# Attention and two expert layers on one core: pairs in column quarters, strays by register addresses, all work by a fixed list

## The chip, the cores and the metric

The kernel runs on 1 core of one Trainium2 chip. The metric is the device time of one execution in microseconds (us). The kernel before takes 580.2 us, the median of 3 runs (579.23 to 580.48).

In this text PE is TensorE, DVE is VectorE, ACT is ScalarE, POOL is GpSimd, SP is SyncE (here it issues nearly all DMAs).

## What is computed

Random-feature attention over 4 batches of 8 heads with 576 tokens, 64 wide, and then two layers of 8 experts, each token to the expert with the largest gate:

```python
def _attn_ref(q, k, v, omega):
    m, D = omega.shape                       # 128 features, 64
    scale = 1.0 / np.sqrt(np.sqrt(D))
    q_s, k_s = (q * scale, k * scale)
    def phi(x):
        proj = np.einsum('bhsd,md->bhsm', x, omega)
        sq = np.sum(x * x, axis=-1, keepdims=True) / 2.0
        h = proj - sq
        h = h - np.max(h, axis=-1, keepdims=True)
        return np.exp(h) / np.sqrt(m)
    q_p, k_p = (phi(q_s), phi(k_s))
    kv = np.einsum('bhsm,bhsd->bhmd', k_p, v)
    z = np.sum(k_p, axis=2)
    num = np.einsum('bhsm,bhmd->bhsd', q_p, kv)
    den = np.einsum('bhsm,bhm->bhs', q_p, z)[..., None] + 1e-06
    return (num / den).astype(np.float32)

def _moe_ref(x, w_gate, w_output_gate, w1, w2):      # x: 2304 x 512, F = 1024, 8 experts
    logits = x @ w_gate
    e_idx = np.argmax(logits, axis=1)
    ...                                              # gate_w: softmax value of the chosen one
    eom = 1.0 / (1.0 + np.exp(-(x @ w_output_gate)))
    for e in range(E):
        mask = e_idx == e
        h = np.maximum(x[mask] @ w1[e], 0.0)
        out[mask] = gate_w[mask, None] * eom[mask, e, None] * (h @ w2[e])
    return out
```

The second layer is the same without the output gate `eom`. The output is the second layer's, kept transposed on the chip as `outT` (512 x 2304).

## The kernel before

**Attention.** A *pair* is two heads of a batch; there are 16, and each has a form (`FORMS`, line 54). All forms project k on 64-row tiles (`k_proj`, line 487): 10 fp32 matmuls, 20 records in the trace, into `ph`; then a maximum (`nm`), and an exponential for each 128 columns (`kp`). q is projected too, its maximum over features is taken by POOL (`partition_all_reduce` into `qhl`), DVE subtracts, ACT takes the exponential. The forms differ in three steps:

- F (5 pairs): `kv` (line 493) as ten fp32 matmuls 128x128, `num` (line 530) as four fp32 matmuls 128x288 into `pa`, features by tokens.
- R (3 pairs): `kv` in four 32-column quarters of the array, 40 matmuls 32x65 into `pkv`; `num` with token rows, again 40 matmuls 32x65 into `pn` (`rows`, line 548), a division by the sum's column, and five transposes `pf` back to features by tokens.
- S (8 pairs): like F, but q and `kv` are cut in a high and a low part in fp32r, and `num` has three terms per half (`qh`·`kvh`, `ql`·`kvh`, `qh`·`kvl`); q's projection takes two terms (`qs` with `omsth` and `omstl`).

In F and S the denominator is a row of `num`; it goes out by DMA to `rdd`, comes back as `rb` on 64 rows, and `norm` multiplies (`xraw<-ev,rb`).

**Expert layers.** Nearly all tokens of a batch choose one expert in each layer. A *unit* is one layer of one batch with its majority expert. `Unit.up` (line 936) has 8 chunks, each 24 fp32r matmuls `pm` (128x288, three terms `xh`·`wh`, `xl`·`wh`, `xh`·`wl`) into one tile of two banks, 576 columns; ACT makes `hh` by relu from all 576 columns, DVE makes the rest `hl`. `Unit.down` (line 963) has 4 chunks of 48 matmuls, whose result DVE multiplies by the tokens' weights `cb` into `y`. 8 units of 384 make 3072 `pm`. The weights come raw as `wr`, ACT casts them to `wh`, DVE makes `wl`, 1024 columns at a time.

**Gates and strays.** Per unit `gate` (line 769) computes logits (`pg`, `pt`), counts (`pc`) and the weights' table (`ptc`, to DRAM as `cohd`). Tokens of another expert than the unit's, the *strays*, are taken by `Block` (line 1035), `JB` = 32 at a time: selection by `sel`, transposes of all tokens (`pst`, `pxt`), a gather by matmul (`pxg`, `pxf`), up (`pu`, `phf`), down (`pyc`), and a scatter by matmul with the table `put` (`pby`). The result `by` is merged into the last unit's `y`, or added to another batch's output (`old`) that is read back. The first block always runs; further ones run in a loop behind the main program, only if the counts ask for it.

**Order.** A planner (`Estimate`, line 102) models each engine's time as the program is written; between the chunks of a unit a `slot` (in `run_unit`, line 1389) lets in the next attention step, gate step or store, by weights, paces and tweaks (lines 58 to 70). Where nothing is ready before the first unit, `fill` issues matmuls `idle` on zeros.

**PSUM.** 8 banks: 7 for attention and 1 for `idle` before the first unit; then two `pm` tiles of two banks and 4 for the rest.

Of the kernel before, what the change touches and what calls it, by code (L numbers as in the profile page):

```python
# [2 lines left out]

# [10 lines left out]
I32 = mybir.dt.int32  # L14
AF = mybir.ActivationFunctionType
# [10 lines left out]
NCH = 5  # L26
# [7 lines left out]
BW = 96  # L34
BN = S // BW
JB = 32
# [13 lines left out]
)  # L50
ORDER = 3


FORMS = "FRRRFFFSFSFSSSSS"
CW = 132
XW = 4

WEIGHTS = (-99.0, -99.0, 465.22, -215.23, 475.57, 303.97, 62.0, -391.59, -72.09, 241.12, -272.33, 415.93, -220.17, 177.53)
RAW_WEIGHTS = (-99.0, -99.0, -320.83, -643.41, 757.51, 23.54, 902.27, -181.77, -108.58, 760.71, -209.95, -1003.88, -544.16, -272.35)
# [40 lines left out]


class Estimate:

    def __init__(self):
        self.now = dict.fromkeys(("tensor", "vector", "scalar", "gpsimd", "sync", "dma"), 0.7)
        self.written, self.used, self.slots, self.before = {}, {}, {}, {}
        self.sums = set()

        self.banks, self.seen, self.uses = {}, {}, 0

        self.window, self.work, self.slow = 0, 0.0, True

        self.holds = []

        self.rows = 128

    def ready(self, tiles):
        return max((self.written.get(t.tensor.name, 0.0) for t in tiles), default=0.0)  # L120

    def tile(self, ring, bufs, t):


        names = self.slots.setdefault(ring, [])
        if len(names) >= bufs:
            old = names[0]
            if self.banks.get(ring):
                read = [n for n in names if n in self.seen and not self.seen[n][1]]
                old = min(read, key=lambda n: self.seen[n][0], default=old)  # L130
            names.remove(old)
            self.before[t.tensor.name] = old
        names.append(t.tensor.name)

    def spare(self, pool, tag):

        ring = id(pool), tag
        return pool.bufs - sum(n not in self.seen or self.seen[n][1] for n in self.slots.get(ring, ()))

    def clock(self, begin):  # L140
        while begin >= (self.window + 1) * 3.413:
            if self.slow:
                self.slow = self.work < 0.77 * 3.413
            else:
                self.slow = self.work < 0.4 * 3.413
            self.window += 1
            self.work = 0.0
        return 2 if self.slow else 1

    def run(self, engine, op, out, ins):  # L150
        n = math.prod((ins[0] if "reduce" in op and ins else out).shape[1:])
        free = self.used.get(self.before.get(out.tensor.name), 0.0)
        begin = max(self.now[engine], self.ready(ins), free)
        psum = any(t.tensor.name in self.sums for t in (out, *ins))
        if op == "dma_start":
            self.now[engine] = begin + (0.42 if out.shape[0] % 128 == 0 else 0.55)
            row = out.shape[-1] * 4
            cost = math.prod(out.shape[:-1]) / 16e3 * (2 + row / 25 if row >= 512 else 40 if row > 256 else 10)
            if len(out.shape) > 2 and row >= 512 or out.shape[0] == 64:
                cost *= 1.5  # L160
            end = self.now["dma"] = max(begin + 1.1, self.now["dma"]) + max(0.17, cost)
            end += 1.0
        elif engine == "tensor":
            if op == "transpose":
                cost, tail = max(n, 128) / 1185, 0.17
            elif ins[-1].dtype == F32:

                cost, tail = 2 * max(2 * n / 2400 + 0.002, 0.111), 0.1
                cost *= 0.5 if ins[-1].shape[0] == 64 else 0.25 if out.shape[0] == 32 else 1
            elif ins[-1].dtype == F32R:  # L170
                cost, tail = n / 2400 + 0.0112, 0.165
            else:
                cost, tail = n / 2400 + 0.0025, 0.165
            rows = 64 if ins[-1].shape[0] == 64 else 32 if out.shape[0] == 32 else 128
            if rows != self.rows:
                begin += 0.1
                cost += 0.107
                self.rows = rows
            cost *= self.clock(begin)
            self.work += cost  # L180
            end = self.now[engine] = begin + cost
            end += tail + 0.045
        else:
            if engine == "gpsimd":
# [4 lines left out]
            elif engine == "vector":  # L189
# [8 lines left out]
                for h in self.holds:  # L198
                    if h < begin < h + 1.2 and not psum:
                        begin = h + 1.2  # L200
# [70 lines left out]

# [1254 lines left out]
```

## Time and profile before

| | |
|---|---|
| median of 3 runs | 580.2 us (579.23 to 580.48) |
| the profiled execution | 578.27 us, its span 576.4 us |
| mean granted PE clock | 0.994 |
| first `pm` starts | 69.03 us |
| last `pm` starts | 569.73 us |
| last store issued | 571.10 us |

The rows come from the one profiled execution; times in them are from the span's start. PE is busy nearly all the time, so its rows are read as a sum of durations by kind of work. A PE row's x counts records: an fp32 matmul leaves two. Records overlap, so the time that a visit costs is taken from one start to the next start.

### The profile page before, as it was taken

Reading aid. Unit: us, or ns where it says so; the run is one execution under the profiler, and the core shown is the slowest. Engines: PE = TensorE matmul, PEld = TensorE weight load, DVE = VectorE, ACT = ScalarE, POOL = GpSimd, SP = SyncE. Lnnn points to the kernel's source line nnn. Section 1 sums busy time; section 2 is a strip of 40 time slices with the busy share of each in tenths; the row PEclk is TensorE's granted clock in tenths of the full one; section 3 lists DMA queues with packets and bytes.
Section 4 is the critical chain, followed back from the end, with each engine's and each line's share of the span. In section 5 each row is a group of like instructions: output and inputs, shape, how many; then the busy total and the mean of one; then the engine's idle time right before and its main releaser. Section 6 shows DMA issues by size and latency. Waiting matters only on the chain.

```text
span 576.4 us, 12103 instructions
## 1 busy us (share of the span) xinstructions
PE 561.6 (97%) x4859; PEld 532.5 (92%) x4859; DVE 365.1 (63%) x685; ACT 222.5 (39%) x503; POOL 68.6 (12%) x48
## 2 busy tenths in 40 slices
PE   8989999999999999999999999999999999999995
PEld 7768789999899999999999999999999999879994
DVE  3696678976976887697686865445544575314522
ACT  5967556332445433522445313312421332224300
POOL 3743400121111111020131000000000000000000
PEclk9989999999999999999999999999999999999998
DMA  8323476636546263373545363533333337964411
GB/s 309 119 85 129 107 233 167 197 98 179 162 116 188 80 200 113 100 241 111 156 118 142 123 196 94 131 135 115 95 115 116 94 96 226 314 204 133 120 42 45
DMA packets 96958, 82.81 MB, mean 144 GB/s; under 512 B 24576, under 2 KB 78464, under 8 KB 96896
## 3 DMA queue, kind: packets, MB, share of 16 engines
q1 hardware_dynamic: 95776, 81.78, 46.6%
q8 instruction: 40, 0.66, 0.5%
q10 hardware_dynamic: 1120, 0.19, 0.2%
q14 instruction: 22, 0.18, 0.1%
HBM read 66.36 MB, written 15.54 MB: 142 GB/s over the span
## 4 chain that ended last, share of the span: by engine, by line
PE 75%; DVE 5%; ACT 1%; issue 1%; ACTq 0%
PE pm L229 62%; PE pa L229 4%; PE pkv L229 3%; PE ph L229 2%; PE pg L229 1%; DVE hl L229 1%; DVE qhh L229 1%; DVE wl L229 1%; PE pby L229 1%; DVE y L229 1%; ACT wh L229 0%; PE pxt L229 0%; ACT hh L229 0%; ACT qhh L229 0%; PE pu L229 0%
## 5 line engine op out<-in xcount | busy, mean ns | idle before, releaser
L229 PE MATMUL pm<-xh,wh 128*128 128x288 f32 x512 | 114.2, 304 | 3.2 <-DVE hl L229 2.0
L229 PE MATMUL pm<-hh,wh 128*128 128x288 f32 x512 | 113.9, 301 | 0.6 <-DVE y L229 0.6
L229 PE MATMUL pm<-hh,wl 128*128 128x288 f32 x512 | 110.8, 295 | 0.0
L229 PE MATMUL pm<-hl,wh 128*128 128x288 f32 x512 | 110.8, 295 | 0.0
L229 PE MATMUL pm<-xh,wl 128*128 128x288 f32 x512 | 109.6, 296 | 0.3 <-DVE wl L229 0.3
L229 PE MATMUL pm<-xl,wh 128*128 128x288 f32 x512 | 109.4, 295 | 0.0
L229 POOL PARTITION_ALL_REDUCE qhl<-qhh x32 | 67.4, 2134 | 242.0 <-DVE qhh L229 167.2
L229 ACT CAST wh<-wr 128x1024 fp32r<-128x1024 f32 (+1 forms) x72 | 68.0, 957 | 69.4 <-PE pm L229 48.7
L229 DVE TENSOR_TENSOR wl<-wr,wh 128x1024 fp32r<-128x1024 f32 (+1 forms) x72 | 78.8, 1104 | 17.2 <-ACT wh L229 16.2
L229 PEld LDWEIGHTS pm<-xh,wh 128*128 128x128 f32 x512 | 81.9, 189 | 7.8 <-DVE hl L229 3.4
L229 PEld LDWEIGHTS pm<-hh,wh 128*128 128x128 f32 x512 | 82.5, 189 | 4.3 <-issue 2.7
L229 DVE SCALAR_TENSOR_TENSOR hl<-pm,hh 128x576 fp32r<-128x576 f32 x64 | 48.3, 754 | 59.6 <-ACT hh L229 58.9
L229 PEld LDWEIGHTS pm<-hh,wl 128*128 128x128 f32 x512 | 82.8, 188 | 0.0
L229 PEld LDWEIGHTS pm<-xh,wl 128*128 128x128 f32 x512 | 82.2, 188 | 0.6 <-DVE wl L229 0.6
L229 PEld LDWEIGHTS pm<-hl,wh 128*128 128x128 f32 x512 | 82.8, 188 | 0.0
L229 PEld LDWEIGHTS pm<-xl,wh 128*128 128x128 f32 x512 | 82.3, 188 | 0.0
L229 ACT ACTIVATE hh<-pm 128x576 fp32r<-128x576 f32 x64 | 41.9, 655 | 73.1 <-PE pm L229 73.0
L229 DVE TENSOR_TENSOR y<-pm,cb 128x576 f32<-128x576 f32 (+1 forms) x33 | 24.2, 732 | 65.7 <-PE pm L229 65.6
L229 ACT ACTIVATE kp<-ph,nm 128x128 f32<-128x128 f32 x140 | 37.7, 392 | 20.2 <-DVE nm L229 20.2
L229 ACT ACTIVATE qhh<-qhh 128x576 f32<-128x576 f32 x32 | 22.5, 719 | 34.7 <-DVE qhh L229 29.6
L229 DVE TENSOR_REDUCE nm<-ph 128x3 f32<-128x384 f32 (+1 forms) x64 | 27.0, 484 | 11.6 <-PE ph L229 9.1
L229 PE MATMUL pkv<-vt,kp 128*128 128x128 f32 (+1 forms) x400 | 32.3, 254 | 0.6 <-issue 0.3
(146 smaller groups left out, 559.0 us busy)
## 6 DMA issues: line engine op xcount, KB each, us to landing
wr<-w2a SPq DMA_DIRECT2D x16, 512.0 KB, 3.8
wr<-w2b SPq DMA_DIRECT2D x16, 512.0 KB, 4.1
qr<-qT SPq DMA_DIRECT2D x24, 288.0 KB, 4.0
wr<-w1a SPq DMA_DIRECT2D x12, 512.0 KB, 4.1
wr<-w1b SPq DMA_DIRECT2D x12, 512.0 KB, 3.8
vt<-vp SPq DMA_DIRECT2D x16, 325.0 KB, 4.6
kr<-kT SPq DMA_DIRECT2D x16, 288.0 KB, 4.0
xd<-xraw SPq DMA_DIRECT2D x16, 288.0 KB, 3.8
```

Source lines behind the costliest of these rows:

```text
L229: return f(*args, **kw)
```

## The change

All 16 pairs take form R, with q projected on 64 rows in fp32, k projected and exponentiated in two parts, and the two-part q, `kv`, and the road over `rdd` gone. A `pm` tile is one bank with 288 columns: each half of the tokens is its own group (`group`, 12 matmuls in up, 24 in down) with its own relu, `hl` or `y`. `psm` keeps two banks, `psa` has six, for the whole program. Some casts of `wh` stand on DVE (names with + in the list): 24 of 1024 columns and 8 of 512. Counts go through a bf16 matmul. `JB` is 8: DVE's maximum of eight finds the stray positions, POOL loads them into registers and copies the eight columns of x; `pu` is 16 matmuls 32x256, `phf` two transposes, `pyc` 32 matmuls 32x128, `pby` one transpose, and POOL copies the eight result columns into a cleared `by`. The planner is gone: `PLAN` is a list of steps, where a number is that many half-groups of the units' matmuls, and a name one step of a pair (its letter, the pair, the half), a gate (`G`), a weight piece (`F` load, `H` cast, `L` rest), or the block (`A`, `B`). There are 25 `idle` matmuls where there were 42.

```diff
-JB = 32
+JB = 8
-FORMS = "FRRRFFFSFSFSSSSS"
+BANKS = 2
...
+def group(nc, out, terms, ws, xs, first, last):
+    for t in terms:
+        nc.tensor.matmul(out, ws(*t), xs(*t), start=first and t == terms[0], stop=last and t == terms[-1])
...
-        def up(self, x, need, slot):
+        def run(self):
...
-                pm = pl.psm.tile([128, 2, 512], F32, tag="pm", name="pm")
...
+                for s in range(2):
+                    pm = pl.psm.tile([128, 512], F32, tag="pm", name="pm")[:, :HS]
+                    for c in (0, 2):
+                        w = self.w[fc // 2]
+                        group(
+                            nc, pm, [(d, *t) for d in (c, c + 1) for t in TERMS],
...
+                    nc.scalar.activation(hh[:, s], pm, AF.Relu)
+                    nc.vector.scalar_tensor_tensor(
+                        out=hl[:, s], in0=pm, scalar=0.0, in1=hh[:, s].bitcast(F32), op0=ALU.max, op1=ALU.subtract
+                    )
+                    yield
...
+            nc.vector.max(out=top, in_=sel)
...
+                t = nc.gpsimd.value_load(at[0:1, j : j + 1], min_val=0, max_val=S)
+                nc.gpsimd.tensor_copy(out=xg[:, :, j : j + 1], in_=x[:, :, bass.ds(t, 1)])
...
+                nc.gpsimd.tensor_copy(out=by[:, :, bass.ds(t, 1)], in_=yw[:, :, j : j + 1])
...
-    psums = ExitStack()
-    pl.psa = pool(psums, "psa", 7, space=PSUM)
-    pl.psi = pool(psums, "psi", 1, space=PSUM)
+    pl.psm = pool(ctx, "psm", BANKS, space=PSUM)
+    pl.psa = pool(ctx, "psa", 8 - BANKS, space=PSUM)
...
+        for name in PLAN.split():
+            if name.isdigit():
+                for _ in range(int(name)):
+                    next(experts)
+            elif name[0] == "z":
+                spin(int(name[1:]))
+            elif name in flows:
+                next(flows[name], None)
```

Of the list, the end:

```
H75 2 L75 3 F77 3 H76+ 2 L76 6 H77 2 L77 1 G7 W7 1 A A A A A A 4 A 2 A 3 A 1 A A A A A A 13 A 5 A A A A A A A A A A A
A B B B B M710 B M700 M720 M730 M731 S710 B B S700 S720 S730 S731 B B B B B
```

PE in the middle of the units, before: an attention visit of an S or F pair (`pkv` sums of k with v, `ph` a projection), between `pm` of a down chunk.

```order
L229 MATMUL pm<-hh,wh 128x288 x2
L229 MATMUL pm<-hl,wh 128x288 x2
L229 MATMUL pm<-hh,wl 128x288 x2
L229 MATMUL pkv<-vt,kp 128x128 x10
L229 MATMUL ph<-om,kr 128x128 x10
L229 MATMUL pm<-hh,wh 128x288 x2
L229 MATMUL pm<-hl,wh 128x288 x2
L229 MATMUL pm<-hh,wl 128x288 x2
```

PE at a like place after (`pn` are the token rows of `num`, `ph<-qr` q's projection):

```order
L92 MATMUL pm<-hh,wh 128x288
L92 MATMUL pm<-hl,wh 128x288
L92 MATMUL pm<-hh,wl 128x288
L242 MATMUL pkv<-vt,kp 32x65 x40
L268 MATMUL pn<-kvr,qhh 32x65 x40
L219 MATMUL ph<-qr,om 128x288 x4
L92 MATMUL pm<-hh,wh 128x288
L92 MATMUL pm<-hl,wh 128x288
```

`kv` and `num` stand there as 40 small matmuls each, and one `pm` at a time goes with a weight piece where there were two.

DVE in the last unit's up, before (`hl` is the rest of relu over 576 columns, `wl` of the weights):

```order
L229 SCALAR_TENSOR_TENSOR hl<-pm,hh 128x576
L229 SCALAR_TENSOR_TENSOR old<-by,state,old 128x576
L229 SCALAR_TENSOR_TENSOR hl<-pm,hh 128x576
L229 TENSOR_TENSOR wl<-wr,wh 128x1024
L229 SCALAR_TENSOR_TENSOR hl<-pm,hh 128x576 x2
L229 TENSOR_TENSOR wl<-wr,wh 128x1024
L229 TENSOR_TENSOR y<-pm,cb 128x576
L229 SCALAR_TENSOR_TENSOR y<-by,state,y 128x576
```

DVE in the last unit's up after:

```order
L516 SCALAR_TENSOR_TENSOR hl<-pm,hh 128x288 x4
L488 TENSOR_TENSOR wl<-wr,wh 128x1024
L516 SCALAR_TENSOR_TENSOR hl<-pm,hh 128x288 x3
L131 CAST wh<-wr 128x1024
L516 SCALAR_TENSOR_TENSOR hl<-pm,hh 128x288
L488 TENSOR_TENSOR wl<-wr,wh 128x1024
L516 SCALAR_TENSOR_TENSOR hl<-pm,hh 128x288 x3
L488 TENSOR_TENSOR wl<-wr,wh 128x1024
```

There are two `hl` of 288 columns for each of 576, a cast of `wh` stands among them, and the additions to `old` have moved out.

PE at the end of the main program, before: the block's `phf` and `pyc` stand at the change from the last but one chunk of work to the last unit's up, with that unit's 384 `pm` around and behind them.

```order
L229 MATMUL phf<-fold_92,u 128x32 x8
L229 MATMUL pm<-hh,wh 128x288 x2
L229 MATMUL pm<-hl,wh 128x288 x2
L229 MATMUL pm<-hh,wl 128x288 x2
L229 MATMUL pm<-xh,wh 128x288 x2
L229 MATMUL pm<-xl,wh 128x288 x2
L229 MATMUL pm<-xh,wl 128x288 x2
L229 MATMUL pyc<-w,h 32x512 x8
```

PE at the end of the main program after (the load of `num` is the test for further blocks):

```order
L92 MATMUL pm<-hh,wh 128x288
L92 MATMUL pm<-hl,wh 128x288
L92 MATMUL pm<-hh,wl 128x288
L701 MATMUL phf<-ident,u 128x128 x2
L713 MATMUL pyc<-w,h 32x128 x32
L721 MATMUL pby<-ident,yc 128x128
L888 TENSOR_LOAD num
```

DVE at the same place after:

```order
L534 TENSOR_TENSOR y<-pm,cb 128x288 x5
L724 TENSOR_TENSOR yw<-pby,xg 128x128
L548 SCALAR_TENSOR_TENSOR y<-by,state,y 128x576
L753 SCALAR_TENSOR_TENSOR old<-by,state,old 128x576
L548 SCALAR_TENSOR_TENSOR y<-by,state,y 128x576 x2
L548 SCALAR_TENSOR_TENSOR y<-by,state,y 128x288 x2
L753 SCALAR_TENSOR_TENSOR old<-by,state,old 128x576 x3
L888 TENSOR_LOAD num
```

The block's second half, its merges and its additions to `old` stand behind the last `pm`, where before only the last half's `y` and merge stood.

## Rows read from the trace of the kernel before

**Rows 1.** The page: busy time of each engine, share of span, instructions.

```profile
PE 561.6 (97%) x4859; PEld 532.5 (92%) x4859; DVE 365.1 (63%) x685; ACT 222.5 (39%) x503; POOL 68.6 (12%) x48
```

**Rows 2.** Windows: stretch, length, busy time per engine, PE clock, DMA share, GB/s.

```profile
0.00:69.00 69.00, 64.66 (x921) 50.76 (x922) 45.22 (x105) 48.99 (x156) 33.46 (x32) 0.98 0.44 145
69.00:340.00 271.00, 267.57 (x2163) 260.52 (x2161) 209.28 (x377) 113.16 (x252) 35.14 (x17) 1.00 0.52 153
```

**Rows 3.** Windows of `pm` alone, a stretch without other work.

```profile
420.00:440.00 20.00, 20.00 (x152) 20.00 (x152) 3.03 (x4) 1.06 (x2) 1.00 0.39 124
```

**Rows 4.** Timeline of PE in the start: start us, duration us, instruction, records.

```profile
4.28 2.51 PE L229 MATMUL ph<-om,kr 64*128 64x128 f32 x20 [0.87 <-DVE om L229]
...
14.06 1.34 PE L229 MATMUL pkv<-vt,pxh 128*32 128x65 f32 x80
...
19.98 1.24 PE L229 MATMUL ph<-qr,om 64*128 64x288 f32 x8
...
43.97 1.35 PE L229 MATMUL pn<-kvr,qhh 128*32 128x65 f32 x80
45.25 0.86 PE L229 MATMUL pf<-ident,xt 128*128 128x128 f32 x5
...
69.03 0.51 PE L229 MATMUL pm<-xh,wh 128*128 128x288 f32 x2
```

**Rows 5.** Waits of PE: whom for, us in total, times, longest.

```profile
PE pm L229 <- DVE hl L229: 2.0, 3, 1.0
```

**Rows 6.** Chain of waits from 107 to 126 us: start, us, what.

```profile
111.54 4.19 PE pm L229 x30
115.74 2.23 PE pkv L229 x20
...
121.37 0.97 PE pa L229 x4
...
123.13 0.54 PE pa L229 x4
```

**Rows 7.** Chain of waits from 486 to 524 us: shares by name, two pieces.

```profile
by line: PE pm L229 60.0%; PE pby L229 10.2%; PE pxt L229 6.9%; PE pu L229 5.2%; PE pyc L229 4.9%; PE pxg L229 4.8%; PE phf L229 4.5%; PE pxf L229 2.1%; PE pst L229 1.7%
...
512.98 1.85 PE pyc L229 x16
...
522.88 1.20 PE pm L229 x9
```

**Rows 8.** Timeline of the end, all engines.

```profile
569.73 0.29 PE L229 MATMUL pm<-hh,wl 128*128 128x288 f32 x1
...
570.55 0.52 DVE L229 SCALAR_TENSOR_TENSOR y<-by,state,y 128x288 f32<-128x288 f32 x1
571.10 0.33 SPq L229 DMA_DIRECT2D outT<-y  x1
```

**Rows 9.** Groups by form, DVE and ACT: count, busy us, mean ns, idle before.

```profile
L229 DVE TENSOR_TENSOR wl<-wr,wh 128x1024 fp32r<-128x1024 f32 x56 | 68.5, 1224 | 12.5 <-ACT wh L229 11.4 <-DMA dt<-xraw 0.5 <-ACTq L1468 0.2
L229 DVE SCALAR_TENSOR_TENSOR hl<-pm,hh 128x576 fp32r<-128x576 f32 x64 | 48.3, 754 | 59.6 <-ACT hh L229 58.9
L229 DVE SCALAR_TENSOR_TENSOR y<-by,state,y 128x576 f32<-128x576 f32 x3 | 2.5, 818 | 0.1
...
L229 DVE TENSOR_TENSOR y<-pm,cb 128x288 f32<-128x288 f32 x2 | 0.9, 458 | 4.5 <-PE pm L229 4.5
...
L229 ACT CAST wh<-wr 128x1024 fp32r<-128x1024 f32 x56 | 58.9, 1051 | 51.6 <-PE pm L229 41.0 <-DMA rb<-rdd 5.3 <-DMA wr<-w1a 2.9
L229 ACT COPY ev<-pa 128x288 f32<-128x288 f32 x26 | 9.8, 440 | 5.6 <-DVE xraw L229 4.7 <-PE pa L229 0.9
```

**Rows 10.** DMA issues: instruction, count, KB each, us to landing.

```profile
outT<-old SPq DMA_DIRECT2D x4, 288.0 KB, 4.2
...
outT<-y SPq DMA_DIRECT2D x2, 144.0 KB, 2.7
```

**Rows 11.** Register loads at the program's test for further blocks: duration ns.

```profile
L1467 POOLq TENSOR_LOAD <-num x1: 484/484/484, 473.2 to 473.2; - x1
```

More of the change, by code (lines that the diff above doesn't have):

```diff
@@ L1 @@
-import math
 from contextlib import ExitStack
+from functools import partial
+from itertools import chain
 import numpy as np
@@ L102 @@
[L102 to L184, printed above, removed]
-                cost, tail = n * (0.0037 if "all_reduce" in op else 0.0024), 0.15
-                if "all_reduce" in op:
-                    begin += 0.12
-                    self.holds = [*self.holds[-7:], begin]
-            elif engine == "vector":
-                fast = not psum and op in ("tensor_copy", "tensor_scalar")
-                if op == "reciprocal":
-                    cost = 0.115 + n * 0.005
-                elif n < 100:
-                    cost = 0.125
-                else:
-                    cost = (n * (0.5 if fast else 1) + 74) / 960
-                tail = 0.083
-                for h in self.holds:
-                    if h < begin < h + 1.2 and not psum:
-                        begin = h + 1.2
-            else:
-                cost = n / 1200 + (0.05 if psum else 0.1) + 0.09 * (len(ins) - 1)
-                tail = 0.11
-            end = self.now[engine] = begin + cost
-            end += tail + 0.04
-        self.uses += 1
-        for t in (out, *ins):
-            name = t.tensor.name
-            self.seen[name] = self.uses, engine == "tensor"
-            self.used[name] = max(end, self.used.get(name, 0.0))
-        self.written[out.tensor.name] = max(end, self.written.get(out.tensor.name, 0.0))
@@ L248 @@
[L248 to L266 removed]
+ORDER = (0, 0), (0, 1), (1, 0), (1, 1), (0, 2), (0, 3), (1, 2), (1, 3)
@@ L779, in gate @@
                 )
-        if l == 0 and not again:
-            kept[0] -= NP
         yield ()
@@ L1128, in prepare @@
-            ps = pl.psa.tile([128, 512], F32, tag="pa", name="pxf")[:, : NDC * JB].rearrange("p (c j) -> p c j", c=NDC)
-            for c in range(NDC):
-                nc.tensor.matmul(ps[:, c], part[:, c * 128 : (c + 1) * 128], fold4, start=True, stop=True)
-            yield [ps]
-            nc.scalar.copy(out=self.xg, in_=ps)
-            yield [self.xg]
+            nc.vector.tensor_scalar(
+                out=back, in0=back, scalar1=-1.0, scalar2=float(S + 2), op0=ALU.mult, op1=ALU.add
+            )
@@ L1161, in up @@
[L1161 to L1168 removed]
+            u = pl.tp.tile([128, 256], F32, tag="u", name="u")
@@ L1354, in store @@
-        def store():
-            while later and est.ready([later[0][0]]) < now["tensor"]:
-                later.pop(0)[1]()
-        def fill():
-            store()
-            if side and soon(side[0]):
-                step()
-            elif not att.go(PACE[4] if side else PACE[5] if pl.psi is None else START_PACE[2]):
-                if pl.psi is not None:
-                    nc.tensor.matmul(idle, zeros[:, 0:128], zeros, start=True, stop=True)
-                else:
-                    now["tensor"] += 0.1
@@ L1445, in attention_moe_moe_kernel @@
-        prepare()
-        while att.n["load_q"] < 3:
-            fill()
-        load_gates()
-        while att.n["kv"] < 2:
-            fill()
-        prepare_gates()
-        for i in range(5):
-            run_unit(i, opens.get(i))
-        assert not waiting and all(p.x is not None for p in pairs)
-        actx.close()
-        pl.tp = pool(ctx, "tp", 1)
-        run_unit(5, 0)
-        block = Block(1)
-        side.append(Stream(ahead(block)))
-        run_unit(6, 0)
-        side.append(Stream(early(block)))
@@ L1467, in attention_moe_moe_kernel @@
+        assert not steps and all(next(f, None) is None for f in (experts, *flows.values()))
     more = nc.values_load(num[0:1, 4:5], min_val=0, max_val=2 * B * E * NB)
```

1097 lines of the change are left out of this document (358 added, 739 removed), and 4 rows, old and new, of the table ORDERS.

## The prediction

> **What bounds the kernel now.** I read the page's busy line first: the reader is to see TensorE (PE) busy for 561.6 of 576.4 us, VectorE (DVE) for 365.1, ScalarE (ACT) for 222.5 [rows 1]. Then the windows, by stage: 69 us before the first MoE matmul, in which PE is at 64.7 and no other engine above 49.0; from 69 to 340 us PE at 267.6 of 271 [rows 2]. So the time is what PE's instructions cost, plus a start that PE shares with ACT and DVE, plus a tail. The MoE matmuls `pm` are 3072, and 152 of them fill 20 us, 0.132 us each [rows 3]: 405.5 us that neither kernel can change. They start at 69.03 [rows 4] and the last begins at 569.73 [rows 8], so they and what lies between them take 501 us. 405.5 is theirs; what stands between is, by the chain of waits, "visits" of PE to attention, gates and strays, which I sum to 86.4 us; 9 us are left for waits and gaps. The list of waits names 2.0 us for the largest, a wait for `hl` [rows 5]. After the last `pm` come 6.4 us: last merge at 570.55, last store at 571.10 [rows 8], its landing and the end.
>
> So there are four terms: start (69.0), visits (86.4), waits and gaps (9), tail (6.4).
>
> **Visits.** Projections of k and gates stay (8 and 7 in the stretch in both kernels). What goes: 8 whole `kv` at 2.23; 8 split q projections of two visits of 0.54; 7 split `num` of 12 records and 3 whole ones of two visits of 0.97 [rows 6]. A record of the split form costs the 0.132 of a `pm` (4 in 0.54), so a split `num` is 1.6. That is 17.8 + 8.6 + 11.1 + 5.8 = 43.3. The block of 32 strays goes too: the shares of its eight names in the chain from 486 to 524 us add to 40.3% of 38 us, 15.3 [rows 7], and with the returns from row-tiled matmuls 16.4. In all 59.7.
> What comes: 8 `kv` and 10 `num` in 32-column quarters, 80 records each. In the start such a `kv` takes 1.34, and after a `num` that began at 43.97 the next work begins at 45.25 [rows 4]: 1.28 each, 23.0. Nine q projections on 64 rows: 8 records took 1.24 [rows 4], of which some 0.06 overlaps with what follows, as with `num`: 10.6 (if the two row halves did not run side by side, two visits of four records at 0.97 [rows 6] are the bound, 17.5). Ten flips of five transposes: 24 transposes `pxt` are 6.9% of 38 us, 0.11 each [rows 7], so five 0.55; in the start a flip took 0.86, 0.79 without an overlap of 0.07 [rows 4]; between these I take 0.66, 6.6. `pu` of the small block stays in the stretch: the same columns as `pyc` of before streamed in 1.85 [rows 7], 2.0. A return: 30 `pm` after a row-tiled visit take 4.19 and not 3.96 [rows 6], 0.2; the order shows 22 such returns where k and gates alone had 15: 1.4. Sum 43.6, so **-16** us, bounds -9 (q one half after the other) and -19 (flips at 0.55, no further return).
>
> **Start.** It is not PE alone. In the new order eight k and seven q projections, eight `kv`, six `num`, six flips and one gate stand ahead of the first `pm`; by the durations above PE has 46.6 us of work, and waits 4.3 for the first data as now [rows 4]. For the same list I get DVE 49.8 (it gains xt, max and casts, and loses the two 64-row multiplications and the cut of q) and ACT 49.8 (exponentials, copies at 0.44, casts) against 45.2 and 49.0 now [rows 2]. PE falls by some 12 and the others don't. The first products begin at 4.28 [rows 4] and ACT gets its first work near 6 us, so below 56 is out of reach; with the same share of idle as now (ACT 49.0 of 69) nothing would be won. I take 61, **-8**, bounds -12 and 0.
>
> **Waits and gaps.** A `pm` tile is now one bank, 288 columns; an up group is 12 matmuls, 1.58 us, and its bank is needed again when the next group ends. ACT's copy of 288 columns takes 0.44, DVE's `y` of 288 0.46 [rows 9], so an evacuation of relu and `hl` is about 1.0 with hops, inside 1.58. Before, it was 0.66 and 0.75 for 576 columns against a group of 24, 3.17. The cover is thinner: a `wl` takes 1.22 and a `wh` 1.05 [rows 9], and in the new DVE order a `wl` or `wh` stands ahead of one `hl` in three or four. The first half finds the engine free, so I charge **+2**, bounds -5 (the list may also close gaps of before) and +25 (the rival below). DVE's work falls in all (24 `wh` casts come, the cuts of q, kv and the two-sided multiplications go), by my sums to about 350 from 365, ACT's to about 190 from 222.
>
> **Tail.** Here the change loses. Before, the block's result is ready at 523 us [rows 7], and after the last `pm` only a multiplication and a merge of 288 columns remain. Now `pu` stands 30 `pm` (4 us) before the end and phf, pyc, pby behind the last `pm`. From there: two transposes and relu 0.9; `pyc`, as many columns as before's 1.85 [rows 7], and its copy, 3.3; `pby` and `yw` 4.0; eight POOL copies to 6.0; then on DVE, one after the other, three merges of 576 and four additions to `old` at 0.82, two merges at 0.52 [rows 8, 9]: 6.7, so 12.7. The last store is one of `old`, 0.36 to issue; the two last stores of before landed after 2.7, those of `old` after 4.2 [rows 10]; I take 3. The end follows by 2.3, as now. 18.4 against 6.4: **+12**, bounds +8 (the POOL copies short) and +15 (landing at 4.2, slower copies).
>
> **POOL's loads.** After `at` is known POOL loads eight registers and copies eight columns while 13 steps of 0.79 us (10.3 us) of `pm` run ahead of `pu`. A load of a register by POOL took 0.48 [rows 11]; a copy of five numbers has no row, between 0.1 and 0.8. So 4.6 to 10.3 us: hidden in the likeliest case, at nothing. PE's `pu` waits for it, and behind `pu` stand the last 30 `pm`; SP issues the block's loads some 35 us before the end.
>
> **Sum.** -8 - 16 + 2 + 12 = -10 on the span of 576.4: 566.4. The profiled execution took 578.3, 1.9 more than its span: 568.3; the median of the runs is 1.9 above the profiled one: **570.2**, forecast 570.
>
> A rule that speaks against the change: the rows show 80 records of quarters in 1.34 us, 17 ns a record [rows 4]. The Trainium skill, page "TensorE: Matmul & The Clock Gate", section "Wait — 56ns, not 53.3ns?", states that start-to-start never drops below about 25 ns however small the matmul. By it the 2560 records that the change runs in quarters would cost 8 to 9 ns more each, some 23 us, and the kernel would take 593. The row disagrees; the page's measurement is of matmuls on the whole array, and the trace decides.
>
> **The rivals.**
> Single banks hold PE (slower): of the 128 up groups some 44 have a `wl` or `wh` of 1.05 to 1.22 us ahead of their `hl`; then relu, `hl` and hops make about 2.0 to 2.3, 0.4 to 0.7 over the 1.58 of a group. At 0.4 us each that is +17: 585. For it: DVE's `hl` already heads the list of waits [rows 5]. Against it: DVE has over a third of its time free. It decides from some 25 such waits on (+10, no gain left).
> The start doesn't shrink, since ACT and DVE at 50 us each and their dependences set it: +8, 578.
> POOL's copies exceed their 10.3 us, say 2 us each: +6, 576.
> The tail is shorter, or the start near its floor: -5, 565.
> Small records cost a floor that these rows don't show: 593.
> The change doesn't do what it says: more strays than eight in a batch, so that the loop behind the list runs, at a pass of over 40 us (16 loads of weights, one block's chain end to end): about 612. The inputs give two strays, so I hold it unlikely.
>
> **How the numbers follow.** Chances: forecast 0.52, single banks 0.15, start 0.13, POOL 0.07, shorter 0.11, floor 0.01, loop 0.01. The forecast's own spread is 564 to 576 by the bounds of the visits and the tail. About 0.2% (1.2 us) is what a measurement of this kernel can tell from no change. Single banks, floor and loop are slower, with a small part of the start's case: 0.18. Within 0.2%: part of the start's case and of few single-bank waits, 0.06. Faster: 0.76. The range 558 to 584 leaves out most of the single-bank case's upper half, the loop and the floor, and a fifth of the short cases.
>
> **What would show it.** First `pm` near 61 (start); `kv` and `num` visits in the chain at 1.28 with 80 records; PE's waits for `hl` and `y` under 5 us in all; 18 us behind the last `pm`, with pyc and seven DVE operations there. It is wrong if quarters cost over 1.6 in the stream, if the list of waits shows PE held by `hl` over ten times, or if the first `pm` stays at 69.

## The result, and the profile after

The changed kernel takes 563.7 us, the median of 4 runs (562.5 to 564.3), against 580.0 for the kernel before in the same comparison: a ratio of 0.9718 (95% interval 0.9698 to 0.9738). The forecast was 570 with a range of 558 to 584.

The profiled execution took 564.31 us, its span is 562.5. It is the slowest of the four, and the profiled one of before (578.27) was faster than all four of its comparison; so the two spans differ by 13.9 us where the medians differ by 16.3. The accounts below are of the spans.

The page's busy line of the kernel after (as in [rows 1]):

```profile
PE 532.2 (95%) x6572; PEld 506.6 (90%) x6572; DVE 347.6 (62%) x778; ACT 190.6 (34%) x484; POOL 74.5 (13%) x68
```

PE works 29.4 us less with 1713 records more. DVE falls to 347.6 and ACT to 190.6 (350 and 190 were said). Windows of the kernel after by stage (columns as in [rows 2]):

```profile
0.00:64.00 64.00, 54.34 (x1428) 43.20 (x1429) 45.65 (x121) 43.87 (x136) 26.75 (x30) 0.97 0.53 174
64.00:340.00 276.00, 272.13 (x3116) 263.40 (x3116) 179.31 (x382) 93.09 (x228) 34.40 (x16) 0.99 0.42 128
...
544.00:563.00 19.00, 2.71 (x69) 2.02 (x67) 6.80 (x11) 0.65 (x2) 1.53 (x8) 0.71 0.51 184
```

The first `pm` starts at 63.86, the last at 543.92. The last window is new: 19 us in which PE works 2.7. The four terms of the sum follow from the starts of first and last `pm`, 405.5 us for the `pm` themselves, and the visits summed from start to start, with the slower first `pm` behind each (the visits of before summed in the same way are 86.4):

| term | before | after | change | said |
|---|---|---|---|---|
| start, to the first `pm` | 69.0 | 63.9 | -5.2 | -8 |
| visits of PE between `pm` | 86.4 | 67.8 | -18.6 | -16 |
| waits and gaps between `pm` | 8.9 | 6.9 | -2.0 | +2 |
| tail, from the last `pm` | 6.7 | 18.6 | +11.9 | +12 |
| span | 576.4 | 562.5 | -13.9 | -10 |

The table counts the tail from the last `pm`'s start, the prediction from its end (6.4 before, 18.3 after).

The visits can be split by what PE does in them. The block of strays falls from 16.4 to 2.1 us, attention from 56.9 to 53.9, gates from 13.1 to 11.9. So 14.3 of the 18.6 are the smaller block, and most of that comes back as the longer tail, +11.9, where the block now ends. In the stretch attention in quarters costs 3.0 less than the mixed forms of before.

PE's waits after (waited for, us in total, times, longest), where [rows 5] had `hl` first:

```profile
PE ph L219 <- DVE om L817: 4.4, 1, 4.4
PE pn L268 <- issue: 2.8, 3, 1.6
PE pm L92 <- issue: 2.5, 1, 2.5
PE pkv L242 <- issue: 2.3, 2, 1.3
PE pm L92 <- DVE hl L516: 1.0, 1, 1.0
```

"issue" is time in which PE waits for nothing that the profile shows. Before had 0.3 us of it, after has 7.6, and the prediction had no term for it.

**The tail**, in the timeline of all engines after the last `pm` (start, duration, instruction):

```profile
544.05 0.38 PE L701 MATMUL phf<-ident,u 128*128 128x128 f32 x2
544.25 0.46 DVE L534 TENSOR_TENSOR y<-pm,cb 128x288 f32<-128x288 f32 x1 [2.74 <-PE pm L92]
544.47 0.38 ACT L703 ACTIVATE h<-phf 128x256 f32<-128x256 f32 x1 [3.94 <-PE phf L701]
544.91 1.95 PE L713 MATMUL pyc<-w,h 128*32 128x128 f32 x64 [0.47 <-ACT h L703]
...
548.12 1.95 POOL L732 COPY by<-yw 128x4 f32 x8 [10.81 <-DVE yw L724]
550.11 0.82 DVE L548 SCALAR_TENSOR_TENSOR y<-by,state,y 128x576 f32<-128x576 f32 x1 [2.13 <-POOL by L732]
550.84 0.81 DVE L753 SCALAR_TENSOR_TENSOR old<-by,state,old 128x576 f32<-128x576 f32 x1
...
551.57 2.40 DVE L548 SCALAR_TENSOR_TENSOR y<-by,state,y 128x576 f32<-128x576 f32 x4
...
553.88 2.27 DVE L753 SCALAR_TENSOR_TENSOR old<-by,state,old 128x576 f32<-128x576 f32 x3
555.46 1.52 SPq L755 DMA_DIRECT2D outT<-old  x3
```

The reader sees one chain with no overlap: `phf` to `pyc`, by `pby` to POOL's eight copies (0.24 us each, issue and all), and then nine DVE operations (five merges into `y`, four additions to `old`), done at 556.2. The last stores and the end take 6.3 more.

### The profile page after: what moved, and what is told of

Its sections match the earlier page's. It is cut to its first block, busy times and chain, and to the rows that moved or that the text cites. A ratio compares the mean times of both kernels' runs of the same rounds, so it can differ in the third digit from the quotient of the medians.

```text
span 562.5 us, 15495 instructions
## 1 busy us (share of the span) xinstructions
PE 532.2 (95%) x6572; PEld 506.6 (90%) x6572; DVE 347.6 (62%) x778; ACT 190.6 (34%) x484; POOL 74.5 (13%) x68
## 4 chain that ended last, share of the span: by engine, by line
PE 91%; DVE 3%; ACT 3%; issue 2%; DMA 1%; POOL 0%; POOLq 0%; DVEq 0%; ACTq 0%
PE pm L92 73%; PE pn L268 4%; PE pkv L242 3%; PE ph L219 3%; PE ph L185 3%; PE pf L304 2%; PE pg L339 1%; ACT kp L199 1%; DMA om<-omst 1%; DVE old L753 1%; DVE y L548 1%; ACT qhh L133 0%; DVE qhh L230 0%; DVE nm L195 0%; PE idle L836 0%
## 5 line engine op out<-in xcount | busy, mean ns | idle before, releaser
L92 PE MATMUL pm<-xh,wh 128*128 128x288 f32 x512 | 152.7, 298 | 3.5 <-issue 2.5
L92 PE MATMUL pm<-hh,wh 128*128 128x288 f32 x512 | 153.7, 300 | 0.0
L92 PE MATMUL pm<-xh,wl 128*128 128x288 f32 x512 | 151.6, 296 | 0.0
L92 PE MATMUL pm<-xl,wh 128*128 128x288 f32 x512 | 151.3, 296 | 0.0
L92 PE MATMUL pm<-hh,wl 128*128 128x288 f32 x512 | 150.9, 295 | 0.0
L92 PE MATMUL pm<-hl,wh 128*128 128x288 f32 x512 | 150.8, 294 | 0.0
L516 DVE SCALAR_TENSOR_TENSOR hl<-pm,hh 128x288 fp32r<-128x288 f32 x128 | 58.5, 457 | 88.7 <-ACT hh L515 88.3
L515 ACT ACTIVATE hh<-pm 128x288 fp32r<-128x288 f32 x128 | 52.8, 413 | 143.1 <-PE pm L92 143.0
L133 ACT CAST wh<-wr 128x1024 fp32r<-128x1024 f32 (+1 forms) x40 | 38.2, 960 | 63.2 <-PE pm L92 57.8
L230 DVE TENSOR_TENSOR qhh<-qhh,qhl 128x576 f32<-128x576 f32 x32 | 30.8, 961 | 1.6 <-POOL qhl L226 1.6
```

Of the source, the lines that this page charges most:

```text
L92: nc.tensor.matmul(out, ws(*t), xs(*t), start=first and t == terms[0], stop=last and t == terms[-1])
L133: nc.scalar.copy(out=out, in_=in_)
L230: nc.vector.tensor_tensor(out=qe, in0=qe, in1=qm, op=ALU.subtract)
L515: nc.scalar.activation(hh[:, s], pm, AF.Relu)
L516: nc.vector.scalar_tensor_tensor(out=hl[:, s], in0=pm, scalar=0.0, in1=hh[:, s].bitcast(F32), op0=ALU.max, op1=ALU.subtract)
```

## Experiments

Each starts from the kernel after; the first six change one point, the last four rearrange more of the list. Ratios are to the kernel before on the same chip; after's own is 0.9718.

### Do the quarters pay, or the 65 columns?

The change turned `kv` from whole matmuls of 128 columns to quarters of 65. Two sizes changed at once. `kv_whole` takes the quartering alone back, in all 16 pairs (three had it before the change):

```diff
-                for g in range(4):
-                    nc.tensor.matmul(
-                        self.pkv[32 * g : 32 * g + 32, w],
-                        self.kp[:, c, j * NF + 32 * g : j * NF + 32 * g + 32],
+                nc.tensor.matmul(
+                    self.pkv[:, w],
+                    self.kp[:, c, j * NF : (j + 1) * NF],
...
```

> kv of every pair as ten fp32 matmuls of 128x65 in place of forty of 32x65; nothing else changes. If a matmul costs by its columns, a visit takes 2.23 x 65/128 = 1.13 us (before's whole form: 2.23 at 128 columns), as much as the quarters' 1.14 to 1.27, and the time stays within 1 us of 563.7, less what the waits named issue (7.6 us in all) owe to the number of instructions: down to 559. Rival, a matmul of 65 columns costs what one of 128 does: 2.23 per visit, +1.0 us for each of 16 pairs: 572 to 580. If the quarters were what the change gains, the second; if the 65 columns were, the first.

`num_whole` does the same to `num` (128 tokens at once in place of four times 32):

> num of every pair as ten fp32 matmuls of 128x65 (128 tokens at once) in place of forty of 32x65. Same two theories: by columns 1.13 us against 1.28, time 558 to 564; by a floor at 128 columns 2.23, +1.0 us per pair: 572 to 580.

Measured: `kv_whole` 571.9 us, 0.9870 (0.9833 to 0.9907); `num_whole` 573.1 us, 0.9887 (0.9852 to 0.9923). Both lose 8 to 10 us. Timeline of PE with `kv_whole` in the start:

```profile
12.62 2.45 PE L241 MATMUL pkv<-vt,pxh 128*128 128x65 f32 x20
```

and with the kernel after:

```profile
12.62 1.34 PE L242 MATMUL pkv<-vt,pxh 128*32 128x65 f32 x80
```

Twenty records of 65 columns take what twenty of 128 took in before's start (2.50 us there, 2.23 in the stretch [rows 6]). So columns below 128 bought nothing here, and against this whole form the four quarters side by side bought all: the second theory, 1.1 us a visit. Why 65 columns cost as much as 128 the runs don't decide: in the whole form of `kv_whole` the loads of weights, 128 columns each, start every 0.112 us, as the matmuls do, so the loads may set the pace, and not a floor of the columns. Nor do these runs compare with before, whose attention visits cost 56.9 us in another form: they tell what form R would cost without quarters.

16 visits at 1.1 would be 17 us, and the runs lost 8 and 9. The visits between `pm` grew from 67.8 to 76.7 with `kv_whole` and to 80.0 with `num_whole`, so 8 and 10 visits there paid 9 and 12. In the start, `kv_whole` moved the first `pm` only from 63.9 to 66.2 with eight longer visits, and `num_whole` moved it to 63.2, earlier, with six. Something came back. Of the term of waits and gaps 6.9 became 2.9 with `kv_whole` and 3.7 with `num_whole`. The waits of PE with `kv_whole` show what went:

```profile
PE ph L219 <- DVE om L816: 4.4, 1, 4.4
PE pm L92 <- DVE hl L515: 2.0, 2, 1.0
PE pyc L712 <- ACT h L702: 0.5, 1, 0.5
```

No wait named issue is left, of 7.6 us; with `num_whole` one of 0.5 is. In the start the `kv` rows of `kv_whole` grew by 8.0 us, PE's waits between rows fell by 4.1, and its other rows took 1.5 less: some 2.3 in all, as measured.

### What is "issue"?

The page's list of DMA queues counts 53 packets of kind "instruction" on queue 8 in the kernel after, 40 in before, 46 with `kv_whole`. They are 16 KB each. Set against the waits of the kernel after (us from the span's start; the packet starts are the trace's DMA records of that kind):

```
packet starts   PE waits from - to    end of wait after packet start
 16.5           17.3 - 18.9           2.4
 23.5           25.0 - 26.0           2.5
 36.0           37.0 - 38.3           2.3
110.0          112.2 - 112.5          2.4
133.6          133.6 - 136.1          2.4
355.0          356.4 - 357.4          2.4
```

All six waits end 2.3 to 2.5 us after a packet has started, and such packets start 3.5 us or more apart. In the other traces of this document 44 more waits of this name end 2.2 to 3.3 us after the latest packet's start, 41 of them at most 2.8. That fits PE running out of instructions: where quarters, gates and projections follow each other, it uses them up faster than they come. The largest wait, in the chain of waits of the kernel after:

```profile
128.76 0.65 PE ph L185 x8
129.41 1.12 PE pg L339 x32
130.53 1.14 PE pkv L242 x80
131.66 1.14 PE pn L268 x80
132.81 0.34 PE pt L348 x2
133.15 0.40 PE pm L92 x3
133.55 2.52 issue
136.07 3.04 PE pm L92 x12
```

There it costs twice. The window from 136 to 139 shows what comes after:

```profile
136.00:139.00 3.00, 2.93 (x13) 2.93 (x13) 0.14 (x1) 1.60 (x6) 0.00 (x0) 0.51 0.62 199
139.00:146.00 7.00, 7.00 (x55) 6.92 (x54) 5.10 (x19) 3.73 (x10) 0.00 (x0) 1.00 0.22 74
```

The granted clock is 0.51 for these 3 us, the lower of the two levels, after PE had stood for 2.5 us; 11 `pm` take 0.24 each and not 0.13, 1.2 us. That does not follow from every such wait: in `warm` (below) PE stands 2.58 us at 130.6, and the granted clock of the 3 us behind it is 1.00. What decides isn't shown. `num_apart` moves one line of the list, so that this `num` stands four steps earlier:

```diff
-G1 1 P1 F10 F11 2 G1 2 G1 G1 e911 ka1 G1 bc G2 v90 v91 H10 L10 G2 ma1 S030 w9 n80 n81 d80 d81 G2 W1 F12 G2 H11 1 ea11
+G1 1 n80 n81 d80 d81 P1 F10 F11 2 G1 2 G1 G1 e911 ka1 G1 bc G2 v90 v91 H10 L10 G2 ma1 S030 w9 G2 W1 F12 G2 H11 1 ea11
```

> The list alone: num and its division of pair 8 stand four steps earlier (at step 60 of the first unit, not at the start of the second among gate, kv and projection). Theory, instructions: PE's wait of 2.5 us at 133.6 us, which the profile puts down to nothing, comes from 106 small matmuls in a row outrunning the loading of instructions; with kv and num apart it goes, and with it the eleven matmuls at the lower clock behind it (1.2 us): 560 to 561. Rival, PE waits there for data of the new unit: the 2.5 us stay, 563 to 564.

Measured: 561.1 us, 0.9674 (0.9636 to 0.9713). The interval just touches that of the kernel after, so the time alone would not settle it; the trace does. No wait of `pm` for issue is left:

```profile
PE pkv L242 <- issue: 2.6, 2, 1.6
PE pn L268 <- issue: 2.1, 3, 1.0
PE pm L92 <- DVE hl L516: 1.1, 2, 1.0
```

No data of the new unit came sooner in this kernel, so the rival falls. Waits and gaps fell from 6.9 to 2.9, the 2.5 and the 1.2 and a little; of these 4.0 us the span kept 1.2, since the first `pm` came 1.3 later and the visits grew by 1.4. Waits named issue are still 4.7 us in all, in quarters. `mix_n0` (below) tried the same in the start.

### How near is a single bank to holding PE?

The prediction's rival on the slower side. `hl_late` lets DVE do one more operation between relu and `hl` in all 128 up groups; its result isn't used:

```diff
                     nc.scalar.activation(hh[:, s], pm, AF.Relu)
+                    nc.vector.tensor_tensor(
+                        out=late, in0=hh[:, s].bitcast(F32), in1=hh[:, s].bitcast(F32), op=ALU.add
+                    )
                     nc.vector.scalar_tensor_tensor(
...
```

> Between relu and hl of each of the 128 up groups DVE does one more operation of 288 columns (about 0.4 us, its result unused), so each bank comes free 0.4 us later. Forecast's theory, an evacuation of about 1.0 us in a cycle of 1.58 has 0.5 to spare: 0 to +4 us on 563.7. Rival, single banks are at their limit: each group pays, 0.4 x 44 to 0.4 x 128, +17 to +50 us.

Measured: 574.0 us (2 runs), 0.9917 (0.9897 to 0.9937): +10.3, between the two. The operation shows 0.46 each and pushes `hl` back by 0.37. From the start of a group's last `pm` to the end of its `hl` the kernel after takes 1.23 us in most groups, 1.29 at the 90th percentile; the bank is needed 1.72 after it (13 `pm`). With `hl_late` it is 1.60 in most, 1.82 to 1.90 where a `wl` is also near. So the forecast's evacuation was right (0.5 us to spare), and of that half microsecond `hl_late` used nearly all. The 30 groups that were then held followed an `hl` that ended 1.8 us or more after its group's last `pm`, 24 of them with a `wl` just ahead on DVE; most waited 0.14 to 0.24 and lost 0.1 more in their first `pm`. Waits and gaps grew from 6.9 to 16.7, the whole loss. PE's list of waits names only 2.4 us of it for `hl`, since most pieces are shorter than the list shows. Why the rival did not come is in the timeline of the kernel after, DVE and ACT around one `wl` in the last unit's up:

```profile
499.69 0.46 DVE L516 SCALAR_TENSOR_TENSOR hl<-pm,hh 128x288 fp32r<-128x288 f32 x1 [1.12 <-ACT hh L515]
500.06 1.22 DVE L488 TENSOR_TENSOR wl<-wr,wh 128x1024 fp32r<-128x1024 f32 x1
500.84 0.41 ACT L515 ACTIVATE hh<-pm 128x288 fp32r<-128x288 f32 x1 [1.19 <-PE pm L92]
501.29 0.46 DVE L516 SCALAR_TENSOR_TENSOR hl<-pm,hh 128x288 fp32r<-128x288 f32 x1
```

DVE has some 1.2 us from one `hl` to the next, and a `wl` of 1.22 fits into this pause: the next `hl` starts as it ends. A `wl` "ahead of" an `hl` in the order costs nothing if it starts right behind the last one. In the whole kernel 6 of 128 `hl` end later than 1.58, and one makes PE wait (1.0 us, at 212 us, where six exponentials stood ahead of a relu).

`casts_act` takes the 32 casts of `wh` on DVE back to ACT (every + at an `H` of the list).

> The 24 casts of wh of 1024 columns and 8 of 512 go back from DVE to ACT (ACT +30 us of work, DVE -20). Theory, neither engine bounds: within 1 us of 563.7. Rival, a 1.05 us cast ahead of a relu delays its bank: 24 x 0.3 to 0.5 us, +7 to +12.

Measured: 565.0 us, 0.9766 (0.9750 to 0.9783), 1.3 us by the medians and 2.8 by the ratios. PE's list of waits is that of the kernel after with no new entry (`hl` 1.0 once), and the `hl` end as early. So the rival falls. Its profiled execution (563.8) is not slower than the one of the kernel after (564.3), so no trace shows where the small loss of the medians sits.

### Is the start set by its first products?

> The list alone: 15 idle matmuls on zeros ahead of the first projection (1.1 to 4.4 us), where the after-kernel's PE does nothing; the first projections ran there at the lower clock (4 records of q in 1.33 us, later 0.76). Theory, the first products stand on the path: with the full clock some 2 us sooner, -1 to -2 us: 562. Rival, ACT and DVE set the start: no change, 563.7 within 0.5.

```diff
-a0 I b0 a1 b1 b2 c0 c1 c2 b3 b4 b5 a2 a3 a4 c3 c4 c5 J q00
+a0 I b0 a1 b1 b2 c0 c1 c2 b3 b4 b5 a2 a3 a4 c3 c4 c5 J z15 q00
```

Measured: 562.9 us, 0.9723 (0.9698 to 0.9748): no difference that this can tell. The first `pm` came 1.6 us earlier, at 62.3, as the theory said. That the first projections had run at the lower clock is read off their durations (12 records of k took 1.49 us there and 0.83 in `warm`); the profile's granted clock is 1.00 in both. But the visits grew to 71.7. The wait of 2.5 us at 133 is still there: it now stands inside the `num` just ahead, from 130.6 to 133.2, and the one at 355 us grew from 1.0 to 1.65. Waits named issue are 7.2 us in all, against 7.6. The 15 matmuls more shift where each packet of instructions ends, which fits that the waits move. This is a hint why single edits of this list are worth less, or more, than their own place shows.

### The tail

`tail_early` moves the block's steps (`A`), the gate's last store, the merges (`M`) and the additions (`B`) in the list; the last lines, cut:

```diff
-H75 2 L75 3 F77 3 H76+ 2 L76 6 H77 2 L77 1 G7 W7 1 A A A A A A 4 A 2 A 3 A 1 A A A A A A 13 A 5 A A A A A A A A A A A
-A B B B B M710 B M700 M720 M730 M731 S710 B B S700 S720 S730 S731 B B B B B
+A 1 A 1 H74 A A 1 A A 1 L74 A A 3 F76 3 H75 2 L75 3 F77 1 A 1 A 1 H76+ A 1 A 1 L76 1 A 5 H77 2 L77 A 1 W7 1 A B B B B
+1 A 1 A 1 A A 1 A A 1 M700 S700 1 B 1 B 2 B 1 B 3 M710 S710 1 B 1 B 2 B 1 B 3 M720 S720 4 M730 S730 3 M731 S731
```

> The list alone: the block's steps from its loads on, the gate's last store, the merges and the additions to old stand earlier; pu at step 22 of the last unit in place of 59, pyc at step 34, all additions inside the unit's down; behind the last pm only y, a merge and a store of 288 columns. Theory, the tail is exposed work: 18.3 us behind the last pm become 6 to 7, and phf, pyc, pby add 2.5 to the stretch: -9, 554 to 556. Rival, the block in the stretch holds up weights and DVE (its 20 loads among the unit's, seven DVE operations among hl and y): half or all of it lost, 559 to 564.

Measured: 556.7 us, 0.9610 (0.9575 to 0.9645), 7 us by the medians. Its end:

```profile
546.18 0.29 PE L92 MATMUL pm<-hh,wl 128*128 128x288 f32 x1
...
547.01 0.52 DVE L548 SCALAR_TENSOR_TENSOR y<-by,state,y 128x288 f32<-128x288 f32 x1
547.56 0.33 SPq L557 DMA_DIRECT2D outT<-y  x1
```

Span 552.7 (the profiled execution, 554.5, is the fastest of five): 6.5 us from the start of the last `pm`, where it was 18.6. The tail was exposed work, and the visits grew by 3.0, of which the block's are 2.4. Part was lost, as the rival had it, at one place, where DVE looks for the strays between two `hl`:

```profile
494.75 0.43 DVE L516 SCALAR_TENSOR_TENSOR hl<-pm,hh 128x288 fp32r<-128x288 f32 x1
495.10 0.45 DVE L641 TENSOR_SCALAR order<-order 128x576 f32<-128x576 f32 x1
...
495.58 0.76 DVE L644 TENSOR_TENSOR sel<-sel,order 128x576 f32<-128x576 f32 x1
...
496.38 0.82 DVE L645 SCALAR_TENSOR_TENSOR sel<-order,state,sel 128x576 f32<-128x576 f32 x1
...
497.23 0.76 DVE L650 MAX8 top<-sel 128x8 f32<-128x576 f32 x1
...
498.31 0.44 DVE L516 SCALAR_TENSOR_TENSOR hl<-pm,hh 128x288 fp32r<-128x288 f32 x1
```

An `hl` comes 3.6 us after the last, and PE's wait for `hl` rises from 1.0 to 2.7 in all. That is the rival of the single banks in one place: here the work ahead of `hl` is longer than the pause.

`mix` puts the search into the last but one unit's down, joins `num_apart`, and lets three of the six exponentials of 212 us stand one step later.

> num_apart and an earlier tail in one list: the strays are found in the last but one unit's down, where DVE has 3.2 us from one y to the next, and not in the last unit's up, where the first early tail held PE 1.7 us for an hl; and of the six exponentials that stand ahead of a relu at step 5 of the third unit, three go one step later (PE waits 1.3 us there). Theory, each wait named goes: 556.7 - 2.6 - 1.9 - 1.1 = 551. Rival, the waits move to the next place: 553 to 556.

Measured: 552.9 us, 0.9552 (0.9536 to 0.9567), nearer to the rival than to the theory: `hl` is down to 0.7 us of waits, no `pm` waits for issue, but quarters wait 6.5 us for it, where they waited 5.3 in `tail_early`.

Two more start from `mix`. `mix_warm` adds the 15 idle matmuls of `warm`; `mix_n0` takes the quarters out of the `num` of the first pair alone:

> mix with the 15 idle matmuls ahead of the first projection. Theory, the start gains 1 to 1.6 us and waits for instructions only move, since 15 more idle matmuls stand ahead of every later load: 552.0 to 552.9. Rival, the earlier clock is worth its 2 us: 551.

> mix with num of the first pair as ten matmuls 128x65 in place of forty of 32x65: 60 PE instructions fewer at the place of the first wait named issue (1.5 us at 17 us). Theory, instructions: that wait goes, the visit costs 1.0 more, and the later waits move or shrink: 551.5 to 553. Rival, that wait is for data (kvr or the exponential): it stays and the visit adds 1.0: 554.

```diff
-                    for g in range(4):
+                    for g in range(0 if self.first and self.hp == 0 else 4):
...
+                    if self.first and self.hp == 0:
+                        nc.tensor.matmul(
+                            ps[:, x, w],
+                            self.q[j][0][:, c0 : c0 + 128],
...
```

`mix_warm`: 551.3 us, 0.9511 (0.9489 to 0.9532), the fastest of all, 5% under the kernel before and 2% under the changed one; it comes out between its theory and its rival. The start gained 0.8; the waits named issue did not only move, they fell from 6.5 to 4.4. `mix_n0`: 556.0 us, 0.9594 (0.9572 to 0.9616), slower than `mix`, as its rival had the time, yet not for its reason. Its wait at 17 us is gone and the first `pm` comes 1.0 us earlier (62.0 to 63.1), though the visit costs 1.0 more:

```profile
16.24 2.45 PE L276 MATMUL pn<-kvr,qhh 128*128 128x65 f32 x20
18.61 1.34 PE L242 MATMUL pkv<-vt,pxh 128*32 128x65 f32 x80
```

But the visits in the stretch grew from 72.4 to 74.6, and the list of waits has 2.3 us for one `num`: with 30 matmuls and their weight loads fewer the later packets fall elsewhere. So the wait was for instructions, and removing it here made others. Together this makes 0.8 us, the difference of the two profiled spans; the medians differ by 3.0, and where the rest sits isn't shown.

## Why the prediction was right, and where its terms were off

The direction, the size within the range, and the mechanisms of visits and tail held. The forecast (570.2) lies 6.5 us above the median. Of these 3.9 are the span's, where errors of +2.8, -2.6 and -4.0 us in start, visits and waits partly cancel, which is luck. The other 2.6 are the step from span to median: 3.8 by the executions of before, 1.2 here.

**Visits: right, 2.6 us too small.** The block gave -14.3 where the sum has 16.4 less 2.0; attention gave -3.0 where it has -1.7, and gates -1.2 where it has nothing. Rows of the start carried over to the stretch: a lone `num` of 80 records took 1.28 there, a q projection 1.17 (1.18 said), a flip 0.64 (0.66 said). Where `kv` and `num` stand together they took 2.42 and not 2.56, as in the chain of waits of the kernel after:

```profile
178.27 1.27 PE pkv L242 x80
179.54 1.14 PE pn L268 x80
180.69 1.17 PE ph L219 x8
```

I had priced each alone. The experiments add what the sum took on trust: form R's price rests on the quarters, 1.1 us a visit, not on the fewer columns. No run takes back the small block or q's projection on 64 rows; their share is read from the rows.

The floor of 25 ns a record did not come: 1.14 us for 80 records are 14 ns each. The Trainium skill, page "TensorE: Matmul & The Clock Gate", section "Wait — 56ns, not 53.3ns?", gives about 25 ns from start to start at the least; this trace does not agree for matmuls on quarters of the array. A cost of small matmuls did exist, but elsewhere: in their number, 7.6 us of waits for instructions, and in this trace the lower clock behind the longest.

**Start: right in kind, too large (-8 said, -5.2 measured).** ACT and DVE were mis-summed as near 50 us each; they were busy 43.9 and 45.7 of the first 64. That error alone would have made the start shorter than forecast, so it isn't what made it longer. Two other terms are: PE's own work was put at 46.6 us, and its rows without `idle`, from start to start, come to 51.5 (the seven q projections 11.7, where 1.18 each makes 8.3); and 4.0 us of waits for issue at 17, 25 and 37 us had no term. Without the first of these waits the start ended 1.0 us sooner, though a visit in it had grown by 1.0 (`mix_n0`). From 40.0 to 43.4 the granted clock is 0.50, and a `num` there took 2.18 where others took 1.35; before has a stretch like it at 36.6. The chain of waits up to the first `pm` is PE for 40 us, ACT for 11, issue for 4.8, DVE for 3.6 and a DMA for 3.4, so neither PE alone nor ACT and DVE set the start. What each term is worth there no run separates.

**Waits and gaps: wrong sign, small (+2 said, -2.0 measured).** The half microsecond to spare was right, by `hl_late` and the 1.23 us measured. The step that failed is the charge for `wl` and `wh` ahead of `hl`: I counted them in the order, and did not see that one placed right behind an `hl` fits into DVE's pause. The term holds 2.5 us of issue and 1.2 us of lower clock at 133 us; where these are gone it is 2.9 (`kv_whole`, `num_apart`), 6 below before's 8.9. Before's list of waits names 3.8 us for `hl`, `y` and `wl`, after's 1.0.

**Tail: right (+12 said, +11.9 measured)**, by its own steps: POOL's copies done 5.9 us after the last `pm`'s end (6.0 said), DVE at 11.9 (12.7 said). That the total is so near is luck: stores and end took 6.3 where 5.7 were said, which nearly cancels DVE's 0.8. That the tail was exposed is shown by `tail_early`.

**POOL's loads** stayed hidden: a load and a copy took 0.70 us, here as in `tail_early`, 5.6 for eight (4.6 to 10.3 said); the copy alone, for which the prediction had no row, took 0.19.

Of the rivals, single banks came in one place (1.0 us) and the start's in part; the others did not come.

## What to carry to other kernels

Price a matmul form by start to start in a row of the same shape, and ask separately how many instructions it takes: a form that is faster per visit can starve PE of instructions where several stand in a row, and the profile then shows a wait for nothing. An engine with a steady pause takes extra work for nothing as long as one piece fits into the pause and starts at its beginning; one piece longer than the pause holds the bank. Ask of work that has left the busy stretch whether it is gone or has only moved: the block's 14 us left the visits here and 12 stood behind the last matmul. So look first at what stands behind the last matmul of the bulk: here moving it forward was worth 7 us on top of the change's 16.

## What the runs showed of the hardware

- An fp32 matmul of 65 columns on the whole array cost what one of 128 columns did: 20 records in 2.45 us, against 2.50 in before's start; the loads of 128 columns of weights started at the same pace, every 0.112 us (`kv_whole`). Four quarters of 65 columns side by side took 1.34 for 80.
- PE's waits without a visible cause ended 2.3 to 2.5 us after the start of a 16 KB instruction packet, six times of six in one trace. With 480 matmuls fewer they were gone (`kv_whole`) or 0.5 us (`num_whole`); with 15 more they moved (`warm`).
- In one trace a wait of 2.5 us was followed by 3 us at a granted clock of 0.51, the lower of its two levels, and 1.00 behind them (the kernel after, 133 us). In another a wait of 2.58 us was not: 1.00 (`warm`, 131 us).
